# Loading the first batch and storing the last batch of a grouped-query attention kernel in pieces

## The chip, the core and the metric

The kernel runs on one core of a Trainium2 chip. The program uses five engines, which run side by side (in the kernel before, PE, DVE, ACT and POOL were each busy for 93 to 95% of the same 840.5 us): PE (matmuls), DVE and POOL (element-wise work), ACT (exponential and scaled copies), and SP, whose queue here only issues DMA transfers and waits for them. The metric is device time in microseconds (us), the median of several executions. In the profiles, `SPq` is the sequencer of SP, `PEld` the weight loads of PE, and `L189` is line 189 of the kernel that was profiled; line numbers shift between kernels, so the same matmul has another line after the change.

## The reference

```python
B, Hq, Hkv, Sq, Sk, D = 16, 32, 8, 288, 512, 128      # bf16
def reference(q, k, v):
    k = jnp.repeat(k, 4, axis=1); v = jnp.repeat(v, 4, axis=1)
    scores = jnp.einsum("bhqd,bhkd->bhqk", q, k) * D ** -0.5
    p = softmax(scores, axis=-1)
    return jnp.einsum("bhqk,bhkd->bhqd", p, v)
```

The kernel works on one batch after the other. A batch has 8 groups (one k/v head and its four q heads); a group has 4 x 288 = 1152 query rows, which are 9 units of 128 rows. So there are 16 x 72 = 1152 units.

## The kernel before

For a unit, PE multiplies 128 query rows with 512 keys (`ps_s`), DVE scales the result and finds the row maximum (`sn_sb`), POOL subtracts it (`x_sb`), PE transposes the result in four blocks (`ps_x`), ACT takes the exponential of two units at a time (`pt_sb`), PE multiplies with V (`ps_o`; a column of ones appended to V gives the sum of the exponentials), DVE forms its reciprocal (`rl_sb`), and ACT or DVE writes the scaled output for three units at a time (`o_sb`). The units are pipelined: PE's queue has the score matmul of unit u, the transposes of unit u-3 and the V product of unit u-8 in turn.

The parts that matter here are the transfers. All are issued by SP, in order:

```python
def op_load_qk(b):
    ...
    eng.dma_start_transpose(qt_sb[:, bb]..., q_v[b]).then_inc(c_ldq.s(b), 16)
    eng.wait_ge(*c_ldq.w(b, 16))                       # q has landed
    eng.dma_start_transpose(kt_sb[:, bb]..., k_v[b]).then_inc(c_ldk.s(b), 16)
    eng.wait_ge(*c_ldk.w(b, 16))                       # k has landed

def op_load_v(b):
    ...
    eng.dma_start(v_sb[:, bb]..., v_v[b]).then_inc(c_ldv.s(b), 16)

def op_store(b):
    if n_oev_act[b]: eng.wait_ge(*c_osta.w(b))         # ACT's last output of the batch
    if n_oev_dve[b]: eng.wait_ge(*c_ostd.w(b))         # DVE's last output of the batch
    eng.dma_start(o_v[b], o_sb[:, bb]...).then_inc(c_out.s(b), 16)
    ...
# PE: the first unit of a batch waits for all of q and k, its first V product for all of V
if u % UPB == 0:
    waits += [c_ldq.w(b, 16), c_ldk.w(b, 16)]
# after the last output op of a batch, one tiny "marker" op raises c_osta or c_ostd
nc.scalar.activation(scr_sb[:, ...], ones_sb[:, 0:1], ACTF.Identity).then_inc(c_osta.s(b), 1)
```

Two buffers alternate, so the load of a batch normally hides behind the work on the one before: in the trace of the kernel before, PE's two waits for a load (17.9 us for k, 0.7 us for V) are both for batch 0. The load of batch 0 and the store of batch 15 have nothing to hide behind (17.86 us before the first matmul, 10.1 us after the last marker).

## Time and profile before

| | |
|---|---|
| time | 842.33 us median of 12 (842.16 to 842.6) |
| span in the profile | 840.5 us |
| first score matmul | 17.86 us |
| first V product | 25.47 us |
| a batch in the middle | 50.1 to 50.6 us |
| last marker to the end of the span | 830.4 to 840.5 us |

The page of the kernel before cuts the span into 40 slices and gives the busy tenths of each; here are PE and the DMA engines.

```profile
PE   1999999999999999999999999999999999999993
...
DMA  8945937497691856839387582766939287681504
```

PE is busy in all slices but the first (a slice is 21 us) and the last. Everything that a change of the first load and the last store can win lies in those two.

The chain of work that ended last, from its start (columns: start, length, what; steps under 0.2 us are left out):

```profile
0.80 10.82 DMA qt_sb<-in_q_dram
11.64 6.18 DMA kt_sb<-in_k_dram
17.89 7.44 DMA v_sb<-in_v_dram
25.47 0.40 PE ps_o L275 x4
25.87 0.21 PE ps_s L189
```

Three transfers stand one behind the other, each starting where the one before has landed. The waits of the kernel before, in us in total, number of times, longest:

```profile
PE ps_s L189 <- DMA kt_sb<-in_k_dram: 17.9, 1, 17.9
...
PE ps_o L275 <- DMA v_sb<-in_v_dram: 0.7, 1, 0.7
```

PE waits once for k, and once more, a little, for V. How busy the engines are in five stretches (head, batch 0, batch 1, batch 15 and tail):

```profile
core 0: us, PE busy (x) PEld busy (x) DVE busy (x) ACT busy (x) POOL busy (x), PEclk, DMA share, GB/s
0.00:17.80 17.80, 0.00 (x0) 0.00 (x0) 0.28 (x2) 1.28 (x1) 0.50 (x5) 1.00 0.89 191
17.80:70.80 53.00, 51.83 (x623) 39.50 (x623) 50.28 (x172) 45.74 (x86) 48.67 (x72) 1.00 0.57 107
70.80:121.10 50.30, 49.82 (x651) 40.39 (x649) 49.67 (x175) 48.83 (x96) 48.68 (x73) 1.00 0.63 137
775.20:830.40 55.20, 52.20 (x679) 41.23 (x676) 50.05 (x177) 52.69 (x104) 48.66 (x72) 1.00 0.20 45
830.40:840.50 10.10, 0.00 (x0) 0.00 (x0) 0.00 (x0) 0.00 (x1) 0.00 (x0) 0.50 1.03 234
```

In a batch four engines are busy for 48.7 to 49.8 of 50.3 us, so there is little to be had in the middle. The end of the timeline of the kernel before, and the sync queue's wait for that transfer:

```profile
830.19 0.21 ACT L349 ACTIVATE scr_sb<-ones_sb 128x1 f32<-128x1 bf16 x1
830.43 0.37 SPq L174 DMA_DIRECT2D out_dram<-o_sb  x1
```

```profile
SPq L391 <- DMA out_dram<-o_sb: 9.2, 1, 9.2
```

The marker ends at 830.4, the store of the whole batch (2.36 MB) is issued, and nothing else happens until 840.5.

### The profile page before, as it was taken

The numbers are of one execution on the slowest core, as the hardware profiler recorded it, in microseconds if no ns is written. First come the engines' busy times: TensorE is split into PE (matmuls) and PEld (weight loads), VectorE is DVE, ScalarE is ACT, GpSimd is POOL, SyncE is SP. The second block draws the span as 40 slices with busy tenths as digits, with TensorE's granted clock in tenths as the row PEclk, the third lists the DMA queues.
The fourth block names the chain that finished last, engine by engine and source line by source line (L and its number), as shares of the span: only waits on it lengthen the run. The fifth ranks groups of instructions, "written<-read, shape, count | busy, mean of one in ns | idle before, by whom it ended". The sixth has DMA issues, their size and how long they took to land.

```text
span 840.5 us, 30405 instructions
## 1 busy us (share of the span) xinstructions
PE 802.6 (95%) x10368; PEld 644.0 (77%) x10368; DVE 795.7 (95%) x2783; ACT 786.0 (94%) x1514; POOL 779.0 (93%) x1157
## 2 busy tenths in 40 slices
PE   1999999999999999999999999999999999999993
PEld 0787888887888787878888878788888888888782
DVE  1999999999999999999999999999999999999992
ACT  0899999999999999999999999999999999999994
POOL 1999999999999999999999999999999999999992
PEclk9999999999999999999999999999999999999997
DMA  8945937497691856839387582766939287681504
GB/s 177 165 88 125 205 68 161 103 165 165 100 206 37 189 130 139 191 71 179 81 165 165 114 192 51 170 134 126 203 69 198 65 165 165 115 192 26 115 2 113
DMA packets 378521, 111.00 MB, mean 132 GB/s; under 512 B 361984, under 2 KB 378368, under 8 KB 378368
## 3 DMA queue, kind: packets, MB, share of 16 engines
q1 hardware_dynamic: 378368, 109.06, 62.5%
q8 instruction: 84, 1.38, 0.7%
q14 instruction: 69, 0.57, 0.2%
HBM read 16.78 MB, written 37.75 MB: 65 GB/s over the span
## 4 chain that ended last, share of the span: by engine, by line
PE 40%; ACT 39%; issue 16%; DMA 3%; ACTq 0%; DVE 0%; SPq 0%
ACT o_sb L339 22%; ACT pt_sb L249 17%; PE ps_o L275 15%; PE ps_x L231 13%; PE ps_s L189 12%; DMA qt_sb<-in_q_dram 1%; DMA v_sb<-in_v_dram 1%; DMA kt_sb<-in_k_dram 1%; ACT scr_sb L349 0%; ACTq L65 0%; DVE rl_sb L294 0%; ACTq L117 0%; SPq L163 0%
## 5 line engine op out<-in xcount | busy, mean ns | idle before, releaser
L214 POOL TENSOR_SCALAR x_sb<-sn_sb,nmx_sb 128x512 bf16<-128x512 f32 x1152 | 778.5, 696 | 45.4 <-DVE sn_sb L202 41.7
L202 DVE TENSOR_SCALAR_CACHE_REDUCE sn_sb<-ps_s 128x512 f32<-128x512 f32 x1152 | 756.7, 680 | 28.9 <-PE ps_s L189 27.5
L249 ACT ACTIVATE pt_sb<-ps_x 128x1024 bf16<-128x1024 bf16 x576 | 595.5, 1074 | 41.4 <-PE ps_x L231 33.1
L275 PE MATMUL ps_o<-v_sb,pt_sb 128*128 128x129 bf16 x4608 | 459.5, 221 | 8.4 <-ACT o_sb L339 2.3
L189 PE MATMUL ps_s<-kt_sb,qt_sb 128*128 128x512 bf16 x1152 | 436.6, 379 | 17.9 <-DMA kt_sb<-in_k_dram 17.9
L231 PE MATMUL ps_x<-ident,x_sb 128*128 128x128 bf16 x4608 | 446.1, 219 | 0.3 <-POOL x_sb L214 0.2
L231 PEld LDWEIGHTS ps_x<-ident,x_sb 128*128 128x128 bf16 x4608 | 325.4, 97 | 141.1 <-POOL x_sb L214 46.1
L275 PEld LDWEIGHTS ps_o<-v_sb,pt_sb 128*128 128x128 bf16 x4608 | 306.3, 98 | 24.9 <-ACT o_sb L339 20.7
L339 ACT ACTIVATE o_sb<-ps_o,rl_sb 128x128 bf16<-128x128 f32 x921 | 283.2, 413 | 1.2 <-DVE rl_sb L294 1.2
L189 PEld LDWEIGHTS ps_s<-kt_sb,qt_sb 128*128 128x128 bf16 x1152 | 113.4, 99 | 19.0 <-DMA kt_sb<-in_k_dram 17.9
L202 DVE DVE_READ_ACCUMULATOR sn_sb<-ps_s 128x1 f32 x1152 | 96.0, 83 | 0.0
L294 DVE RECIPROCAL rl_sb<-ps_o 128x3 f32<-128x3 f32 x384 | 67.5, 176 | 3.6 <-PE ps_o L275 3.6
L330 DVE TENSOR_TENSOR o_sb<-ps_o,rl_sb 128x384 bf16<-128x384 f32 x77 | 42.6, 553 | 0.0
L349 ACT ACTIVATE scr_sb<-ones_sb 128x1 f32<-128x1 bf16 x16 | 4.3, 271 | 0.0
L249 ACT ACT_TABLE_LOAD x1 | 1.3, 1283 | 1.8 <-POOL ident L378 1.8
L378 POOL TENSOR_SCALAR_AFFINE_SELECT ident<-ones_sb 128x128 bf16<-128x128 bf16 x1 | 0.3, 295 | 0.9 <-DVE v_sb L402 0.9
L401 DVE MEMSET ones_sb<- 128x128 bf16 x1 | 0.2, 165 | 0.9 <-PEq L424 0.9
L347 DVE MEMSET scr_sb<- 128x1 f32 x16 | 0.9, 59 | 0.0
L424 POOL MEMSET const-float32-0.0<- 128x1 f32 x1 | 0.1, 99 | 0.3 <-issue 0.3
L402 DVE MEMSET v_sb<- 128x64 bf16 x1 | 0.1, 112 | 0.2 <-issue 0.2
L424 POOL MEMSET const-bfloat16-1.0<- 128x1 bf16 x1 | 0.1, 102 | 0.0
L424 POOL MEMSET const-uint8-127<- 128x1 uint8 x1 | 0.1, 102 | 0.0
(1 smaller groups left out, 0.1 us busy)
## 6 DMA issues: line engine op xcount, KB each, us to landing
out_dram<-o_sb SPq DMA_DIRECT2D x16, 2304.0 KB, 15.7
qt_sb<-in_q_dram SPq DMA_TRANSPOSE x16, 12.2
kt_sb<-in_k_dram SPq DMA_TRANSPOSE x16, 7.1
v_sb<-in_v_dram SPq DMA_DIRECT2D x16, 0.2 KB, 7.5
```

The costliest lines, as they stand in the source:

```text
L189: emit(eng, waits, lambda: eng.matmul(ps_s[:, u % NSB, :], qt_sb[:, bb, gl, t, :], kt_sb[:, bb, gl].rearrange("p j c -> p (j c)"), start=T ...
L202: emit(eng, waits, lambda: eng.tensor_scalar(out=sn_sb[:, u % NS, :], in0=ps_s[:, u % NSB, :], scalar1=-scale, scalar2=None, op0=ALU.mult, ...
L214: emit(eng, waits, lambda: eng.tensor_scalar(out=x_sb[:, u % NX, :], in0=sn_sb[:, u % NS, :], scalar1=-1.0, scalar2=nmx_sb[:, u % NM:u % N ...
L231: ins = emit(eng, w, lambda: eng.transpose(ps_x[:, c % NXB, slot, j, :], x_sb[:, u % NX, j * P:(j + 1) * P], ident[:]))
L249: emit(eng, waits, lambda: eng.activation(pt_sb[:, c % NPB, 0:n].rearrange("p a j c -> p (a j c)"), ps_x[:, c % NXB, 0:n].rearrange("p a j ...
L275: ins = emit(eng, w, lambda: eng.matmul(ps_o[:, r % 2, oslot * DV:(oslot + 1) * DV], pt_sb[:, c % NPB, slot, j, :], v_sb[:, bb, gl, j, :], ...
L294: emit(eng, waits, lambda: eng.reciprocal(rl_sb[:, r % NR, 0:n], src.rearrange("p a e -> p (a e)"))).then_inc(c_rc.s(r), 1)
L330: emit(eng, waits, lambda: eng.tensor_tensor(out=o_sb[:, bb, gl, t0:t0 + n, :], in0=src_o, in1=rl_sb[:, r % NR, 0:n].unsqueeze(2).broadcas ...
L339: ins = emit(eng, w, lambda: eng.activation(o_sb[:, bb, gl, t0 + i, :], ps_o[:, r % 2, i * DV:i * DV + D], ACTF.Identity, scale=rl_sb[:, r ...
L347: nc.vector.memset(scr_sb[:, b % 2:b % 2 + 1], 0.0).then_inc(c_ostd.s(b), 1)
L349: nc.scalar.activation(scr_sb[:, 4 + b % 2:5 + b % 2], ones_sb[:, 0:1], ACTF.Identity).then_inc(c_osta.s(b), 1)
L424: nc = _bacc.Bacc("TRN2", target_bir_lowering=False, num_devices=1)
```

## The change

The intent: start the work as soon as the first group has been loaded, and store each group of the last batch as soon as it is done, so that only one eighth of the store comes after the last output. The diff, cut to its core:

```diff
+        PG = [0, 1, 2, 4, 8]                  # groups: pieces of 1, 1, 2 and 4
+        def op_load_first(i):
+            g0, g1 = PG[i], PG[i + 1]
+            sq, sk, sv = first_sems(i)
+            eng.dma_start_transpose(qt_sb[:, 0, g0:g1]..., q_v[0, g0*NT*P:g1*NT*P]).then_inc(sq, 16)
+            eng.dma_start_transpose(kt_sb[:, 0, g0:g1]..., k_v[0, g0*NJ*P:g1*NJ*P]).then_inc(sk, 16)
+            if i == 0:
+                eng.wait_ge(s_init, 1)
+            eng.dma_start(v_sb[:, 0, g0:g1]..., v_v[0, :, g0*NJ:g1*NJ]).then_inc(sv, 16)
+            if i == len(PG) - 2:
+                for s in (sq, sk, sv):
+                    eng.wait_ge(s, 16)
...
-            if u % UPB == 0:
+            if b == 0:                        # PE, score matmul: wait for this piece of q and k
+                if u % NT == 0 and g in PG[:-1]:
+                    fs = first_sems(PG.index(g))
+                    waits += [(fs[0], 16), (fs[1], 16)]
+            elif u % UPB == 0:
                 waits += [c_ldq.w(b, 16), c_ldk.w(b, 16)]
...                                            # the V product likewise, for this piece of V
+        NPC = 8
+        GPP = G // NPC
+        def op_store(b, piece=None):          # last batch: wait for this piece's markers, then
+            g0, g1 = piece * GPP, (piece + 1) * GPP
+            eng.dma_start(o_v[b, :, g0*NT:g1*NT], o_sb[:, bb, g0:g1]...).then_inc(c_out.s(b), 16)
...                                            # markers of the pieces of the last batch
+                if last_in_piece and pc < NPC - 1:
+                    if oev_on_dve(r):
+                        nc.vector.memset(scr_sb[:, 16+pc:17+pc], 0.0).then_inc(s_pcd[pc], 1)
+                    else:
+                        nc.scalar.activation(scr_sb[:, 8+pc:9+pc], ones_sb[:, 0:1], ACTF.Identity).then_inc(s_pca[pc], 1)
```

Two things change in the head at once: the load is split, and the waits between its transfers are gone. The rest of the diff makes constants configurable with unchanged values, widens `scr_sb` from 8 to 32 columns to hold the markers, and adds an argument for half loads that is never used.

More of the change, by code (lines that the diff above doesn't have):

```diff
@@ L7 @@
 ACTF = mybir.ActivationFunctionType
+CFG = {}
 BF16 = mybir.dt.bfloat16
@@ L40, in bass_standalone__gqa_softmax__near_ridge_kernel @@
     v_v = v.rearrange("b g s d -> b (g s) d").rearrange("b (c p) d -> b p c d", p=P)
-    NSB = 3
-    NXB = 3
-    NS = 3
-    NX = 4
-    NPB = 4
-    assert NS >= NSB and NSB + NXB + 2 <= 8
+    NSB = CFG.get('NSB', 3)
+    NXB = CFG.get('NXB', 3)
+    NS = CFG.get('NS', 3)
+    NX = CFG.get('NX', 4)
+    NPB = CFG.get('NPB', 4)
     NM = 8
     NR = 2
-    XPB = 2
-    LAG_XT = 3.0
-    LAG_PV = 8.0
-    OE_PERIOD = 5
-    OE_DVE = (2,)
+    XPB = CFG.get('XPB', 2)
+    assert NS >= NSB and NSB + NXB * ((XPB + 1) // 2) + 2 <= 8
+    LAG_XT = CFG.get('LAG_XT', 3.0)
+    LAG_PV = CFG.get('LAG_PV', 8.0)
+    OE_PERIOD = CFG.get('OE_PERIOD', 5)
+    OE_DVE = CFG.get('OE_DVE', (2,))
     n_xc = (U + XPB - 1) // XPB
@@ L70, in bass_standalone__gqa_softmax__near_ridge_kernel @@
         kt_sb = es.enter_context(nc.sbuf_tensor("kt_sb", [P, 2, G, NJ, P], BF16))
-        scr_sb = es.enter_context(nc.sbuf_tensor("scr_sb", [P, 8], FP32))
+        scr_sb = es.enter_context(nc.sbuf_tensor("scr_sb", [P, 32], FP32))
         sn_sb = es.enter_context(nc.sbuf_tensor("sn_sb", [P, NS, FREE], FP32))
@@ L105, in bass_standalone__gqa_softmax__near_ridge_kernel @@
         c_exp = Chan("exp", max(NPB, NXB))
-        c_pv = Chan("pv", max(2 * NPB - 1, OPB + 1))
+        c_pv = Chan("pv", max(XPB * (NPB - 1) + 1, OPB + 1))
         c_rc = Chan("rc", NR)
@@ L111, in bass_standalone__gqa_softmax__near_ridge_kernel @@
         s_init = es.enter_context(nc.semaphore("s_init"))
+        s_q0a = es.enter_context(nc.semaphore("s_q0a"))
+        s_pca = [es.enter_context(nc.semaphore("s_pca%d" % i)) for i in range(7)]
+        s_pcd = [es.enter_context(nc.semaphore("s_pcd%d" % i)) for i in range(7)]
+        s_ldp = [[es.enter_context(nc.semaphore('s_ldp%d_%d' % (i, j))) for j in range(3)] for i in range(3)]
+        s_k0a = es.enter_context(nc.semaphore("s_k0a"))
         s_c0 = es.enter_context(nc.semaphore("s_c0"))
@@ L141, in sp_drain, with op_load_qk @@
             del sp_plain[:]
-        def op_load_qk(b):
+        GH = G // 2 if G >= 2 else 0
+        def op_load_qk(b, part=None):
             eng = nc.sync
@@ L148, in op_load_qk, with first_sems @@
                 eng.wait_ge(*c_qkfree.w(b - 2))
+            if part is None:
+                g0, g1 = 0, G
+            elif part == 0:
+                g0, g1 = 0, GH
+            else:
+                g0, g1 = GH, G
+            sq = s_q0a if part == 0 else c_ldq.s(b)
+            sk = s_k0a if part == 0 else c_ldk.s(b)
+            nq = 16 if part == 0 else c_ldq.w(b, 16)[1]
+            nk = 16 if part == 0 else c_ldk.w(b, 16)[1]
             eng.dma_start_transpose(
-                qt_sb[:, bb].rearrange("d g t p -> d (g t p)"), q_v[b]).then_inc(c_ldq.s(b), 16)
-            eng.wait_ge(*c_ldq.w(b, 16))
+                qt_sb[:, bb, g0:g1].rearrange("d g t p -> d (g t p)"),
+                q_v[b, g0 * NT * P:g1 * NT * P]).then_inc(sq, 16)
+            eng.wait_ge(sq, nq)
             eng.dma_start_transpose(
-                kt_sb[:, bb].rearrange("d g j p -> d (g j p)"), k_v[b]).then_inc(c_ldk.s(b), 16)
-            eng.wait_ge(*c_ldk.w(b, 16))
+                kt_sb[:, bb, g0:g1].rearrange("d g j p -> d (g j p)"),
+                k_v[b, g0 * NJ * P:g1 * NJ * P]).then_inc(sk, 16)
+            eng.wait_ge(sk, nk)
+        PG = [0, 1, 2, 4, 8]
+        assert PG[-1] == G
+        def first_sems(i):
+            if i == len(PG) - 2:
+                return c_ldq.s(0), c_ldk.s(0), c_ldv.s(0)
+            return tuple(s_ldp[i])
+        def op_load_first(i):
+            eng = nc.sync
+            g0, g1 = PG[i], PG[i + 1]
+            sq, sk, sv = first_sems(i)
+            eng.dma_start_transpose(
+                qt_sb[:, 0, g0:g1].rearrange("d g t p -> d (g t p)"),
+                q_v[0, g0 * NT * P:g1 * NT * P]).then_inc(sq, 16)
+            eng.dma_start_transpose(
+                kt_sb[:, 0, g0:g1].rearrange("d g j p -> d (g j p)"),
+                k_v[0, g0 * NJ * P:g1 * NJ * P]).then_inc(sk, 16)
+            if i == 0:
+                eng.wait_ge(s_init, 1)
+            eng.dma_start(
+                v_sb[:, 0, g0:g1].rearrange("p g j e -> p (g j) e")[:, :, 0:D],
+                v_v[0, :, g0 * NJ:g1 * NJ]).then_inc(sv, 16)
+            if i == len(PG) - 2:
+                for s in (sq, sk, sv):
+                    eng.wait_ge(s, 16)
         def op_load_v(b):
@@ L165, in op_load_v @@
             sp_plain.append(c_ldv.w(b, 16))
-        def op_store(b):
+        NPC = 8
+        GPP = G // NPC
+        def op_store(b, piece=None):
             eng = nc.sync
             bb = b % 2
-            if n_oev_act[b]:
-                eng.wait_ge(*c_osta.w(b))
-            if n_oev_dve[b]:
-                eng.wait_ge(*c_ostd.w(b))
-            eng.dma_start(o_v[b], o_sb[:, bb].rearrange("p g t d -> p (g t) d")).then_inc(c_out.s(b), 16)
-            sp_plain.append(c_out.w(b, 16))
+            if piece is None or piece == NPC - 1:
+                if n_oev_act[b]:
+                    eng.wait_ge(*c_osta.w(b))
+                if n_oev_dve[b]:
+                    eng.wait_ge(*c_ostd.w(b))
+            else:
+                if piece_has[(False, piece)]:
+                    eng.wait_ge(s_pca[piece], 1)
+                if piece_has[(True, piece)]:
+                    eng.wait_ge(s_pcd[piece], 1)
+            if piece is None:
+                g0, g1 = 0, G
+            else:
+                g0, g1 = piece * GPP, (piece + 1) * GPP
+            eng.dma_start(
+                o_v[b, :, g0 * NT:g1 * NT],
+                o_sb[:, bb, g0:g1].rearrange("p g t d -> p (g t) d")).then_inc(c_out.s(b), 16)
+            if piece is None:
+                sp_plain.append(c_out.w(b, 16))
         def op_s(u):
@@ L265, in op_pv @@
             waits = []
-            if u % UPB == 0:
+            if b == 0:
+                if u % NT == 0 and g in PG[:-1]:
+                    waits.append((first_sems(PG.index(g))[2], 16))
+            elif u % UPB == 0:
                 waits.append(c_ldv.w(b, 16))
@@ L311, in bass_standalone__gqa_softmax__near_ridge_kernel @@
                 n_oev_act[bq] += 1
+        piece_has = {(kd, pc): False for kd in (False, True) for pc in range(8)}
+        for r in range(n_oc):
+            g_ = grp_of(oc_units(r)[0])
+            if g_ // G == B - 1 and NPC > 1:
+                piece_has[(oev_on_dve(r), (g_ % G) // GPP)] = True
         def op_oev(r):
@@ L344, in op_oev @@
                                for r2 in range(r + 1, min(n_oc, r + UPB)))
+            if b == B - 1 and NPC > 1:
+                pc = gl // GPP
+                last_in_piece = all(oev_on_dve(r2) != oev_on_dve(r) or grp_of(oc_units(r2)[0]) // G != b
+                                    or (grp_of(oc_units(r2)[0]) % G) // GPP != pc
+                                    for r2 in range(r + 1, min(n_oc, r + UPB)))
+                if last_in_piece and pc < NPC - 1:
+                    if oev_on_dve(r):
+                        nc.vector.memset(scr_sb[:, 16 + pc:17 + pc], 0.0).then_inc(s_pcd[pc], 1)
+                    else:
+                        nc.scalar.activation(scr_sb[:, 8 + pc:9 + pc], ones_sb[:, 0:1], ACTF.Identity).then_inc(s_pca[pc], 1)
             if last_of_kind:
@@ L356, in bass_standalone__gqa_softmax__near_ridge_kernel @@
         for b in range(B):
-            add("sp", 3 * b + 0, (lambda b=b: op_load_qk(b)))
-            add("sp", 3 * b + 1, (lambda b=b: op_load_v(b)))
-            add("sp", 3 * (b + 2) + 2 if b + 2 < B else 3 * B + b, (lambda b=b: op_store(b)))
+            if b == 0 and GH:
+                for i in range(len(PG) - 1):
+                    add("sp", -1.0 + 0.1 * i, (lambda i=i: op_load_first(i)))
+            else:
+                add("sp", 3 * b + 0, (lambda b=b: op_load_qk(b)))
+                add("sp", 3 * b + 1, (lambda b=b: op_load_v(b)))
+            if b == B - 1 and NPC > 1:
+                for pc in range(NPC):
+                    add("sp", 3 * B + b + 0.1 * pc, (lambda b=b, pc=pc: op_store(b, pc)))
+            else:
+                add("sp", 3 * (b + 2) + 2 if b + 2 < B else 3 * B + b, (lambda b=b: op_store(b)))
         for u in range(U):
@@ L390, in _ @@
             for sl in range(min(2, B)):
-                eng.wait_ge(c_out.sems[sl], 16 * ((B - sl + 1) // 2))
+                tot = 16 * ((B - sl + 1) // 2)
+                if (B - 1) % 2 == sl:
+                    tot += 16 * (NPC - 1)
+                eng.wait_ge(c_out.sems[sl], tot)
         @block.tensor
```

## The prediction

> **What bounds the kernel now.** Three stretches of the 840.5 us span (measured 842.44 us: about 1.9 us lie outside it).
>
> 1. Head. The chain of waits gives q's transposed load of batch 0 from 0.80 for 10.82 us, then k's from 11.64 for 6.18 us; the first score matmul starts at 17.86. V is issued at 17.89 and takes 7.44 us: the first ps_o matmul starts at 25.47, PE having waited 0.7 us for V.
> 2. Middle. 16 batches at 50.27 us each; the table of stretches has PE busy about 49.8 of these, DVE 49.6, ACT 48.9, POOL 48.6: all balanced, DMA share 0.63 to 0.71. The change does not touch this.
> 3. Tail. The last ACT marker ends at 830.4; the 2.36 MB store of batch 15 is issued at 830.43, its data flow at 290 GB/s from 831.4 to 839.6, and the span ends at 840.5. Nothing else runs.
>
> **What the change does.** It loads batch 0 in pieces of 1, 1, 2 and 4 groups (q, k, V per piece, no wait between), stores batch 15 in 8 pieces, and adds 7 small marker ops on ACT and up to 7 memsets on DVE in the last batch.
>
> *Head.* From the two full loads: (10.82-6.18) us for 1.31 MB more is about 282 GB/s, with about 2.5 us fixed. Their issue takes 8.72 us for 9216 rows and 4.17 for 4096, so about 0.5 us fixed and 0.9 ns per row (estimate): 1.5 us for the first q piece (1152 rows), 1.0 for k (512). So k issues at about 2.3 and lands 2.5+0.5 us later: first score matmul near 5.2 instead of 17.86, a gain of 12.7 us. V lands near 7, before the first ps_o matmul wants it (about 7 us after the start): 0.7 us more. Later pieces (estimate) land near 8.5, 13 and 20, wanted near 12.5, 18.5 and 31. The slow first matmuls (0.63 us instead of 0.38 for about 6.4 us) are moved, not removed[...].
>
> *Tail.* Only the last eighth, 0.295 MB, follows the last marker: 8.15/8 = 1.0 us of data plus the same 1.9 us fixed: 3.0 us instead of 10.1, a gain of 7.1. [...] The earlier pieces come 6.3 us apart and need about 3: no queue.
>
> *Cost.* Existing ACT markers take 0.21 to 0.34 us (median 0.30), DVE's 0.06. Seven are 2.1 us on ACT, which has some 1.4 us free in a 50.27 us batch: about 1.0 us lost, 0.3 to 2.
>
> Nearly all of this is on the critical path: at both ends nothing else runs.
>
> **Sum.** 842.4 - 12.7 - 0.7 - 7.1 + 1.0 = about 823 us; range 820.5 to 826.5. Two per cent is 825.6, close: faster by over 2% 0.82, within 2% 0.17, slower 0.01.
>
> **What would show it.** First score matmul at 4.8 to 6; no PE wait on V or later pieces; batches of 50.3 us unchanged; last batch longer by about 1 us; last marker to end about 3 us.
>
> **What would make it wrong.** If transposed loads do not overlap on the queue and each pays its fixed 2.5 us, the start slips to about 7 and piece 2 arrives late: 825 to 827. If ACT paces the last batch, its markers cost 2 us. If small pieces lose bandwidth, the tail keeps 4 us. If the middle shifts its phase, some us either way.

## The result and the profile after

| | before | after |
|---|---|---|
| time, median | 842.33 us (12 runs) | 821.66 us (8 runs, 821.21 to 822.34) |
| span in the profile | 840.5 us | 819.5 us |
| first score matmul | 17.86 | 4.95 |
| first V product | 25.47 | 10.75 |
| batch 0 (first POOL op of batch 0 to first of batch 1) | 51.53 | 49.72 |
| batches 1 to 14, together | 704.35 | 704.35 |
| last batch (start of its first POOL op to start of the last reciprocal) | 54.02 | 54.24 |
| last marker to the end | 10.13 | 3.59 |

The ratio is 0.9755, with a 95% interval of 0.9746 to 0.9765. Ratios here are the mean time of one kernel's fast runs over that of the other's of the same rounds, so not quite the ratio of the medians.

The slices of the page after:

```profile
PE   7999999999999999999999999999999999999996
...
DMA  9878677483975818769186592857939388483522
```

PE's first slice has gone from 1 to 7, its last from 3 to 6. The sync queue's part of the timeline after (start, length of the issue, line, what):

```profile
0.80 1.28 SPq L188 DMA_TRANSPOSE qt_sb<-in_q_dram  x1
2.14 1.24 SPq L191 DMA_TRANSPOSE kt_sb<-in_k_dram  x1
3.43 0.58 SPq L196 DMA_DIRECT2D v_sb<-in_v_dram  x1
4.07 1.42 SPq L188 DMA_TRANSPOSE qt_sb<-in_q_dram  x1
```

and the start of the chain (steps under 0.1 us left out):

```profile
0.80 1.28 SPq L188
2.14 2.77 DMA kt_sb<-in_k_dram
4.95 0.62 PE ps_s L256
```

The transfers now follow one another with 0.04 to 0.06 us between SP's issues, and the chain has the landing of one small k piece in place of three whole transfers. Of the waits listed above only this is left; PE waits for no V and for no later piece:

```profile
PE ps_s L256 <- DMA kt_sb<-in_k_dram: 5.0, 1, 5.0
```

The stretches after (head, batch 0, batch 1, batch 15, tail), with the columns of the table before:

```profile
0.00:4.90 4.90, 0.00 (x0) 0.00 (x0) 0.28 (x2) 1.28 (x1) 0.50 (x5) 1.00 0.41 93
4.90:56.10 51.20, 50.65 (x623) 38.10 (x623) 49.95 (x172) 45.76 (x86) 48.58 (x72) 1.00 0.87 167
56.10:106.40 50.30, 49.82 (x650) 40.47 (x648) 49.66 (x175) 48.83 (x95) 48.68 (x74) 1.00 0.69 139
760.50:815.90 55.40, 52.22 (x679) 41.21 (x676) 50.06 (x181) 53.21 (x111) 48.64 (x72) 1.00 0.36 82
815.90:819.50 3.60, 0.00 (x0) 0.00 (x0) 0.00 (x0) 0.00 (x0) 0.00 (x0) 0.69 0.37 84
```

Batch 1 is what it was. The end, with the sync queue's last wait:

```profile
815.69 0.21 ACT L435 ACTIVATE scr_sb<-ones_sb 128x1 f32<-128x1 bf16 x1
```

```profile
SPq L488 <- DMA out_dram<-o_sb: 2.7, 1, 2.7
```

So the 21.0 us of span are 12.9 at the start, 1.8 in batch 0, 6.5 in the tail, less 0.2 in the last batch (12.9 + 1.8 + 6.5 - 0.2 = 21.0). The prediction had 12.7, 0.7, 7.1 and -1.0. Three of the four terms were off by 0.6 to 1.1 us. Two of these errors helped (V by 1.1, the markers by 0.8) and one hurt (the tail by 0.6), so they cancelled in part and left 1.5 us of span with the 0.2 at the start. The experiments ask two questions: do the two ends gain what the theory says, and why are the three terms what they are?

One line of the transfer view of the tail after (815 to 820 us) stands out:

```profile
q1 hardware_dynamic: 1168, 0.29, 26.0%
q14 instruction: 1, 0.01, 0.9%
...
out_dram<-o_sb SPq DMA_DIRECT2D x1, 288.0 KB, 3.1
```

Beside the 1168 packets of the last store there is one packet of another queue, 8 KB that the profile calls instruction traffic. It took 0.68 us on its engine, and the store's last packets, moving at 18 GB/s, end 0.6 us after the rest. The last store lands after 3.07 us; the four that came just before it, without an 8 KB packet among theirs, took 2.42 to 2.57 us. (The expectations below call it an instruction fetch on a DMA ring; what the trace shows is the name of the queue, the packet's size and its time.)

### The profile page after: what moved, and what is told of

Read it like the earlier page. It is cut to its first block, busy times and chain, and to the rows that moved or that the text cites. A ratio compares the mean times of both kernels' runs of the same rounds, so it can differ in the third digit from the quotient of the medians.

```text
span 819.5 us, 30439 instructions
## 1 busy us (share of the span) xinstructions
PE 801.5 (98%) x10368; PEld 642.6 (78%) x10368; DVE 795.4 (97%) x2787; ACT 786.5 (96%) x1521; POOL 778.9 (95%) x1157
## 4 chain that ended last, share of the span: by engine, by line
PE 41%; ACT 41%; issue 17%; POOL 0%; DMA 0%; SPq 0%; DVE 0%; ACTq 0%
ACT o_sb L415 22%; ACT pt_sb L316 18%; PE ps_o L345 15%; PE ps_x L298 14%; PE ps_s L256 12%; POOL x_sb L281 0%; DMA kt_sb<-in_k_dram 0%; SPq L188 0%; DVE sn_sb L269 0%; ACT scr_sb L435 0%; ACT scr_sb L430 0%; ACTq L66 0%; DVE rl_sb L364 0%; ACTq L123 0%
## 5 line engine op out<-in xcount | busy, mean ns | idle before, releaser
L435 ACT ACTIVATE scr_sb<-ones_sb 128x1 f32<-128x1 bf16 x16 | 4.3, 271 | 0.0
L430 ACT ACTIVATE scr_sb<-ones_sb 128x1 f32<-128x1 bf16 x7 | 2.0, 280 | 0.0
```

The source lines that it names most:

```text
L430: nc.scalar.activation(scr_sb[:, 8 + pc:9 + pc], ones_sb[:, 0:1], ACTF.Identity).then_inc(s_pca[pc], 1)
L435: nc.scalar.activation(scr_sb[:, 4 + b % 2:5 + b % 2], ones_sb[:, 0:1], ACTF.Identity).then_inc(c_osta.s(b), 1)
```

## The experiments

Twelve kernels ran, all correct. Their times are medians; the kernel before had 842.39, 842.44 and 842.21 us in the three sets of runs.

### 1. The head alone and the tail alone

`e1_head_only` sets `NPC = 1`; `e2_tail_only` loads batch 0 as before.

```diff
-        NPC = 8
+        NPC = 1                               # e1_head_only
...
-            if b == 0 and GH:
+            if False:                         # e2_tail_only, with PE's old waits for batch 0
```

> The change's piecewise load of batch 0, but the last batch stored whole. Theory (two independent gains, at the head and at the tail): the head is worth 14.7 us as the trace of the changed kernel shows (batch 1 starts 14.72 us earlier), so 842.3 - 14.7 = 827.6 us, and the tail from last marker to end is 10.1 us again. Rival (the shifted phase of the middle or a hidden interaction gives part of it): outside 826.6 to 828.6.

> The change's eight stores of the last batch, but batch 0 loaded whole as before. Theory: 6.5 us gained after the last marker, 0.2 us lost to the markers, so 842.3 - 6.3 = 836.0 us; with the head-only kernel the two gains add up to the whole change within 0.7 us. Rival: if the 3.6 us that remain after the last marker come from an instruction fetch that happened to fall on the last store, this kernel, whose last store falls elsewhere, has 3.0 us there and 835.4 us.

Measured: the head alone 827.79 us (ratio 0.9829, interval 0.9814 to 0.9844), the tail alone 836.04 (0.9924, 0.9908 to 0.9941). The gains are 842.39 - 827.79 = 14.6 and 842.39 - 836.04 = 6.35 us; together 20.95, where the whole change gained 842.33 - 821.66 = 20.67. The two ends are independent within 0.3 us. The rival's number for the tail (835.4) failed, since it took the packet to have fallen there by chance: the packet is in this kernel's last store too (0.31 us long), which landed after 3.28 us. That the packet is the cause is not refuted by this; experiments 4 and 5 come back to it.

### 2. Splitting without the removed waits, and the waits removed without splitting

`e3_whole_no_wait` has one piece of 8 groups, its three transfers issued without waits; its tail is the old one. `e4_pieces_waiting` is the changed kernel with a wait after each of the twelve first transfers.

```diff
-        PG = [0, 1, 2, 4, 8]
+        PG = [0, 8]                           # e3_whole_no_wait, with NPC = 1
```
```diff
             eng.dma_start_transpose(qt_sb[...], q_v[...]).then_inc(sq, 16)
+            eng.wait_ge(sq, 16)               # e4_pieces_waiting; likewise after k and V
```

> Batch 0 loaded in one piece, q, k and V issued one after the other without the waits between; the last batch stored whole. Separates the removed waits from the splitting. Theory (the fixed part of a load, 2.5 us, is paid once when loads queue): k lands at about 0.8 + 2.5 + 3.41 MB / 282 GB/s = 15.4 instead of 17.8, V near 21, before the first ps_o matmul wants it: 2.4 us at the start and about 1 from V, so about 839 us. Rival (queued transposed loads do not overlap): first score matmul at 17.9, and only V comes earlier: 841.5 us.

> The changed kernel with a wait for the landing after each of the twelve first loads, as the old code had between its three. Theory: pieces are only worth their price because they queue. From the landings in the changed kernel's trace (3.6, 2.8, 2.9 us for a piece of one group) the start slips to about 7.2, the second piece's k lands near 16.5 where it is wanted near 13.6, the third's near 28 where it is wanted near 23: about 2.2 + 2.9 + 5 = 10 us lost, so about 832 us, with PE waits for k of pieces two and three. Rival (the splitting is what counts, waits are cheap): loses only the 2.2 us at the start, 824 us.

Measured: 839.30 us (0.9963, 0.9948 to 0.9978) and 832.64 (0.9884, 0.9869 to 0.9899), both near the theory and away from the rivals. In the chain of `e3_whole_no_wait`, k is issued when q's issue is done, and before q has landed at 11.9:

```profile
0.80 8.74 SPq L188
9.53 0.06 issue
9.59 6.40 DMA kt_sb<-in_k_dram
15.99 0.05 issue
16.04 0.62 PE ps_s L256
```

So the two transposed loads do overlap, from 9.6 to 11.9 us, but what that saves is only 1.8 us at the start (first score matmul at 16.04 in place of 17.86): q's issue alone takes SP 8.74 us, and 3.4 MB must still come. The longest waits for data of `e4_pieces_waiting`:

```profile
PE ps_s L256 <- DMA kt_sb<-in_k_dram: 13.4, 4, 6.4
```

PE waits for k four times, once for each piece, as against once after the change. Taking off the tail's 6.35 us, splitting alone gains 842.39 - 832.64 - 6.35 = 3.4 us, removing the waits alone 3.1, and both 14.6. What small pieces win was eaten here by the part of a transfer's time that does not shrink with its size, since the pieces did not queue up: alone, a q piece of 0.295 MB took 3.08 us and a k piece of 0.131 MB took 2.47 here (by these two about 2.0 us of each would be fixed, an estimate).

### 3. Why batch 0 became 1.8 us shorter, not 0.7

Two suspects: the wait for V, and the slow matmuls at the start (0.63 us in place of 0.38). `e7_before_v_early` is the kernel before, with V issued right behind k. The warm kernels put throwaway matmuls on PE while it waits for the first load: in the trace of the kernel before, the slow score matmuls were the first nine, up to 24.51 us, and my guess, which no trace had shown, was that other matmuls run before them would be the slow ones in their place.

```diff
-            eng.wait_ge(*c_ldk.w(b, 16))
+            if b > 0:                         # e7_before_v_early
+                eng.wait_ge(*c_ldk.w(b, 16))  # for b = 0, k's landing is waited for after V's issue
```
```diff
             eng.wait_ge(s_init, 1)
+            for _i in range(22):              # e5_after_warm; 220 in the two kernels made from before
+                eng.matmul(ps_o[:, 0, 0:P], ident[:], ones_sb[:], start=True, stop=True)
```

> The kernel before with V of batch 0 issued right behind k, without waiting for k's landing; nothing else. Theory: V lands about 3 us earlier, the first ps_o matmul no longer waits for it and comes at about 24.7: 0.7 us gained, 841.6 us; the slow matmuls then show. Rival (V's wait explains all of the 1.81 us that batch 0 lost): 840.5 us.

> The changed kernel with 22 throwaway matmuls on PE before the first load lands[...]. Theory: batch 0 takes 1.81 us less in the changed kernel than before; part of that is the slow stretch of the first matmuls, 3.4 us long there and 6.4 us before. What is left of it costs the changed kernel 0.3 to 1.0 us, so 820.7 to 821.4 us, and the run to run spread (821.2 to 822.3) shrinks. Rival (the slow stretch is hidden behind DVE and costs nothing): 821.7 us, no change.

> The kernel before with 220 throwaway matmuls on PE during its head. Theory (V, landing at 25.34, binds there, and hides the slow matmuls): 842.3 us, no change within 0.3, the first ps_o matmul still at 25.47. Rival (the slow matmuls cost the kernel before the 1 us or more that batch 0 lost): about 841.2 us.

> Both: V early and 220 throwaway matmuls, in the kernel before. Theory (V's wait and the slow matmuls hide one another): more than the sum of the two single edits, the whole 1.8 us or a little over, 840.3 us. Rival (the two are independent): the sum of the gains of the two single runs.

Measured: `e7_before_v_early` 841.02 us (0.9980, 0.9967 to 0.9992): the edit gained 1.42 us, nearer to the rival than to my 0.7. (PE still waited 0.2 us for V in it, and its first score matmul came 0.3 us later than before, so the wait was worth a little more.) `e5_after_warm` 821.71 (no change), `e6_before_warm` 845.69 and `e8_before_v_early_warm` 844.48: slower than before, which neither side expected.

The warm kernels failed as experiments: the score matmuls were slow at the start all the same. In `e6_before_warm` PE ran 220 matmuls in 14.05 us, and was then idle for 5.2 us before the first score matmul: by the trace's record the granted clock fell to 0.50 at 18.8 us, 3.0 us after the last throwaway matmul, and the score matmuls began at 21.0. In `e5_after_warm` the 22 matmuls took 2.5 us, and the first score matmul came 1.0 us after them: full clock is on record only from 10.1 us, 4.8 us after the first score matmul. And in both long ones the first loads were later; see the last section. So they do not tell the two suspects apart as planned. But the traces together go far towards it. The length of batch 0, by the number of slow score matmuls (over 0.5 us) at its start (`e4_pieces_waiting`, where PE waits for k within batch 0, is left out):

| V | kernel: slow matmuls, batch 0 in us |
|---|---|
| late (lands 7.5 us after k) | e2_tail_only: 5, 51.71; e6_before_warm: 7, 51.61; before: 9, 51.53 |
| early | e9_markers_x4: 5, 49.64; after: 5, 49.72; e1_head_only: 6, 49.83; e3_whole_no_wait: 6, 49.97; e7_before_v_early: 6, 50.08; e11_tail_3: 7, 49.86; e12_tail_4: 7, 49.91; e8_before_v_early_warm: 7, 49.99; e5_after_warm: 7, 50.00; e10_after_again: 8, 50.45 |

With V late, batch 0 takes 51.5 to 51.7 us whatever the number of slow matmuls: the first V product comes 7.6 to 7.8 us after the first score matmul, when V has landed. With V early it takes 49.6 to 50.5; five slow matmuls go with the shortest and eight with the longest, though six and seven are not in order. The prediction read the wait for V off one trace in which nine matmuls were slow; PE reached the V product late by itself there, and only 0.7 us were left to wait. In the other two executions with V late PE is there earlier and waits longer: 1.8 us in `e2_tail_only` (five slow matmuls) and 1.6 in `e6_before_warm` (seven). The wait for V and the slow stretch hid one another, and removing V's wait was worth 1.1 to 1.9 us, by the length of the slow stretch (51.6 - 50.5, 51.6 - 49.7). It would also account for the larger spread of the changed kernel (1.1 us, as against 0.4 before, in the runs of the result): the slow stretch differs between executions, and now nothing hides it. These last steps are read from one trace per kernel; no run fixed the number of slow matmuls.

From the timeline of `e10_after_again`, PE's first score matmuls and the last slow one before the V product:

```profile
5.13 2.01 PE L256 MATMUL ps_s<-kt_sb,qt_sb 128*128 128x512 bf16 x4 [5.13 <-DMA kt_sb<-in_k_dram]
...
10.29 0.63 PE L256 MATMUL ps_s<-kt_sb,qt_sb 128*128 128x512 bf16 x1
...
11.70 0.40 PE L345 MATMUL ps_o<-v_sb,pt_sb 128*128 128x129 bf16 x4
```

Here matmuls are slow until 10.9 us, 5.8 us after the first, and eight of them are slow where 5 to 7 were expected; in the trace of the changed kernel above it was 3.2 us. The slow stretch goes with the record of the granted clock in the traces: full clock is on record from 24.40 us in the kernel before, 8.28 after the change and 11.36 in `e10_after_again`, each within 0.5 us of the end of the last slow matmul (24.51, 8.19 and 10.93). What the clock was before that is not on record in the traces before and after the change (the PEclk column of the stretches counts such time as 1.00). Why the number of slow matmuls varies (five to nine in the table), and with it the length of the stretch (3.23 us after the change, 6.65 in the kernel before), is not shown.

### 4. What the markers cost

`e9_markers_x4` issues four marker ops where the change has one (28 in place of 7). To hold them it also widens `scr_sb` from 32 to 64 columns, which the cut below leaves out.

```diff
+                        for _i in range(3):
+                            nc.scalar.activation(scr_sb[:, 32+3*pc+_i:33+3*pc+_i], ones_sb[:, 0:1], ACTF.Identity)
                         nc.scalar.activation(scr_sb[:, 8+pc:9+pc], ones_sb[:, 0:1], ACTF.Identity).then_inc(s_pca[pc], 1)
```

> The changed kernel with four ACT marker ops per piece in place of one (21 more, about 0.3 us each in the trace). The changed kernel lost only 0.22 us in the last batch where 1.0 was predicted. Theory (ACT has slack in the last batch, and a marker overlaps its neighbours so that it takes 0.1 to 0.2 us of ACT's time): 21 more use up the slack and cost 1 to 3 us, 822.7 to 824.7 us. Rival A (each marker costs its full 0.3 us): 6.3 us, 828 us. Rival B (ACT is not on the critical path at all there): no change, 821.7 us.

Measured: 821.64 us (0.9755, 0.9742 to 0.9768), where the unchanged kernel in the same set had 821.38 (0.9752). By time alone this is no difference: rival B's number, where the theory had 822.7 to 824.7; rival A (828 us) is excluded. The trace shows more. Of its groups of instructions on ACT:

```profile
L431 ACT ACTIVATE scr_sb<-ones_sb 128x1 f32<-128x1 bf16 x21 | 3.3, 290 | 0.0
```

21 ops of 290 ns each on average cover only 3.3 us, since they overlap. The last batch takes 55.43 us, 1.19 more than the 54.24 after the change and 1.41 more than the 54.02 without markers. Two kernels without split stores (before, e1_head_only) have 54.02, three with eight stores (after, e2_tail_only, e4_pieces_waiting) 54.24, and the two with fewer pieces 54.12 and 54.13. So seven markers (with four DVE memsets) cost 0.22 us, and 28 cost 1.4, about 0.03 to 0.05 us each. The time did not show it, because two other things gave it back. The last store landed after 2.42 us, free of the instruction packet, and the tail was 0.65 us shorter. And batches 1 to 14 took 703.64 us, 0.71 less than the 704.35 of the change, about 0.05 us in each batch; every other trace has 704.30 to 704.37. Nothing in those batches was edited; the wider `scr_sb` moves the tiles behind it in memory, and no run tests whether that is why. With 0.24 us lost at the start and 0.08 gained in batch 0, the two spans are equal (819.5 us). That these offset is read from one trace.

### 5. The last store

`e10_after_again` is the changed kernel once more. `e11_tail_3` stores the last batch in pieces of 6, 1 and 1 groups. `e12_tail_4` cuts the last group into two thirds and one third.

```diff
-        NPC = 8
-        GPP = G // NPC
+        PB = [0, 18, 21, 24]                  # e11_tail_3, in thirds of a group
+        PB = [0, 18, 21, 23, 24]              # e12_tail_4
+        NPC = len(PB) - 1
+        def piece_of(r):
+            return max(i for i in range(NPC) if PB[i] <= r % (UPB // OPB))
```

> The changed kernel unchanged, for its spread and for what recurs in its trace: 821.7 us again. Theory: the small instruction fetch packet on one DMA ring falls into the last store again, about 2.5 us before the end, because it hangs on the place in the instruction stream, and the last store takes 3.0 to 3.1 us to landing where the earlier free ones take 2.4. Rival: it was chance, and this trace has 2.4 us. The number of slow score matmuls at the start varies from run to run (5 to 7).

> The changed kernel with the last batch stored in three pieces of 6, 1 and 1 groups in place of eight: the last store is the same 288 KB, but the sync queue has five stores less and ACT five markers less to do. Theory (the instruction fetch comes where the added instructions put it): no fetch packet in the last store, which lands after 2.4 us in place of 3.07, and 0.1 to 0.2 us less for markers: about 820.9 us. Rival (the last store is slower because the final wait or the end of the program makes it so): 3.0 us to landing again, 821.5 us.

> Four pieces: 6 groups, 1 group, two thirds and one third of the last group, so that only 96 KB are stored after the last marker. Theory (1.9 to 2.0 us fixed and 290 GB/s): 1.5 + 0.34 + 0.3, that is 1.8 to 2.1 us to landing if nothing delays a ring, so 0.4 us less than the kernel with three pieces: about 820.5 us. If the store of two thirds of a group, issued about 2.4 us before, is still under way, the gain is smaller. Rival: the time to landing is all fixed, no gain.

Measured: 821.38, 821.06 and 820.10 us (0.9752, 0.9748 and 0.9739). The transfer views of the three tails, in this order:

```profile
q1 hardware_dynamic: 1168, 0.29, 28.9%
q14 instruction: 1, 0.01, 0.8%
...
out_dram<-o_sb SPq DMA_DIRECT2D x1, 288.0 KB, 2.9
```

```profile
q1 hardware_dynamic: 1168, 0.29, 42.0%
...
out_dram<-o_sb SPq DMA_DIRECT2D x1, 288.0 KB, 2.4
```

```profile
q1 hardware_dynamic: 400, 0.10, 14.1%
...
out_dram<-o_sb SPq DMA_DIRECT2D x1, 96.0 KB, 1.7
```

The packet recurs where the kernel is unchanged, and with the same 288 KB store it is gone in `e11_tail_3`, which lands after 2.44 us; there the packet comes 1.8 us after the end. All five kernels with eight stores and single markers (after, its repeat, e2_tail_only, e4_pieces_waiting, e5_after_warm) have it, 2.2 to 2.6 us before the end. Its place goes with the number of instructions issued, not with the transfer, and the rival of `e11_tail_3` (the final wait makes the last store slow, 3.0 us again) fell. `e11_tail_3` changes the instructions of both SP and ACT, `e9_markers_x4` (also free of it) those of ACT alone. In that trace the packet comes 12.2 us before the end in place of 2.5, while the three 8 KB packets before it, from 779 us on, lie within 0.9 us of where the changed kernel has them. So it goes with ACT's instruction stream; no view names its engine.

`e12_tail_4` is the fastest version: all its timed runs (820.06 to 820.81) lie below all those of the changed kernel in the same set (821.29 to 821.98), about 1.3 us less at the median. From last marker to end it takes 2.26 us. Its rival (the time to landing is all fixed) fell: 1.74 us for 96 KB, as against 2.44 for 288 KB.

## Why the prediction was right, point by point

- **Time.** Predicted 823.0 (820.5 to 826.5), measured 821.66. Right, with the edge of two per cent as close as it said: a ratio of 0.9755. The two large terms (12.7 and 7.1 us) carry it. That the sum came within 1.3 us is in part luck: the errors of +1.1, +0.8, +0.2 and -0.6 us in the terms partly cancelled.
- **First score matmul.** Predicted near 5.2, measured 4.95. The step "k lands 2.5+0.5 us later" came out as 2.77 us. That pieces only win when they queue, which this step took for granted, was shown by `e4_pieces_waiting`, 11.0 us slower than the change. The alternative that the prediction named under what would make it wrong, loads that do not overlap, was shown false by `e3_whole_no_wait` (k issued at 9.59 us, q landed at 11.9).
- **V, "0.7 us more".** Mis-sized: 1.8 us in the profiled run (whose slow stretch was one of the shortest; 1.1 to 1.9 over the traces), 1.42 us with that edit alone. The wait for V was read from one trace in which slow matmuls hid part of it. "Moved, not removed" held in kind; the length of the slow stretch, 6.65 us before and 3.23 after, is not a constant.
- **Later pieces.** Predicted to land (k) near 8.5, 13 and 20; the trace has 8.48, 14.03 and 24.01, each before it was wanted. No new wait. The last one was 4 us later than estimated, and harmless.
- **Middle.** Predicted unchanged: batches 1 to 14 take 704.35 us in both traces.
- **Tail, "3.0 us instead of 10.1".** The mechanism was right; the trace has 3.59. The 0.6 us go with a packet of instruction traffic within the last store; `e11_tail_3`, without it, has 2.96. The "1.9 us fixed" of the prediction runs from the last marker to the end of the span; from a store's issue to its landing only 1.4 to 1.5 us of it are left (an estimate from three stores, last section).
- **Markers, "about 1.0 us lost".** Mis-sized: 0.22 us. The trace had given the length of a marker (0.3 us), not the time it takes from its neighbours; 28 of them cost 1.4 us, by one trace.

## What to carry to other kernels

At the two ends of this kernel nothing hid a transfer (17.86 us before the first matmul, 10.1 us after the last marker), and the change at both gained 20.7 us. In a kernel with such ends, split the first load so that work can start on its first piece, and the last store so that little follows the last output. Splitting and queueing belonged together here: a wait after every piece gave back 11.0 us of the change's 20.7. Before costing a removed wait, ask what else was slow at the same time: here the wait for V showed 0.7 us in the trace with nine slow matmuls and 1.8 in one with five. And the length of an op in a profile was not what it took from an engine whose ops overlapped: markers of about 0.3 us cost 0.03 to 0.05 each.

## What the traces show of instruction packets, fixed times and the slow start

- At the two ends of this kernel, where nothing hides a transfer, transfers with an instruction packet within them took longer; the page counts their time with that of the data, as a share of the same 16 DMA engines (0.2% for the 8 KB packets and 0.7% for those of 16 KB over the whole run before). Eleven 288 KB stores, over six traces, with one 8 KB packet that began 0.9 to 1.6 us after their issue landed after 2.75 to 3.28 us (in the trace after the change 3.07 us with the packet at 1.04 and 2.87 with it at 1.59), those with no instruction packet after 2.42 to 2.45. The time goes with the place of the packet. In the trace of the kernel before, five k loads with no packet, or only one that began within 0.2 us of the issue or before it, took 6.14 to 6.18 us; of the eleven with a later one, ten took 6.87 to 8.25 and one 6.22. In `e6_before_warm`, a 16 KB packet fell within each of the first two loads, which took 12.39 and 7.75 us in place of 10.82 and 6.18: the kernel with the throwaway matmuls was 3.3 us slower (their effect other than by instruction traffic was not tested apart).
- For stores from SP the runs give 1.4 to 1.5 us (estimate) to landing beyond the data at the 290 GB/s of the store before, at three sizes: 9.60 us for 2.36 MB, 2.43 for 0.295 MB and 1.74 for 0.098 MB. For transposed loads two sizes, twice each in `e4_pieces_waiting` (2.47 and 2.46 us for 0.131 MB, 3.08 and 2.96 for 0.295 MB), give about 2.0 us and 270 to 330 GB/s (estimate), and SP was busy for 1.28 and 1.24 us to issue the first two pieces after the change.
- The slow score matmuls lasted 3.2 to 6.65 us from the first. With 22 throwaway matmuls over 2.5 us before them (`e5_after_warm`) full clock was on record 4.8 us after the first score matmul; without them it was 3.3 us after it in one trace of the changed kernel and 6.2 in the other.
